# A fused FFT and SwiGLU kernel: the order of mirrored gate, gate, value and output matmuls within a unit

## The chip, the cores and the metric

The kernel runs on one core of a Trainium2 chip. The metric is the device time of one execution in microseconds (us); the time of a kernel is the median of its runs.

## The reference

The input `x` is 8 batches of 3008 rows of 256 numbers. The reference takes the real part of a two-dimensional FFT over the rows and the columns of each batch, and feeds the resulting 24064 rows to a SwiGLU block with 256 inputs, 1536 hidden units and 256 outputs:

```
attn = fft(fft(x, axis=1), axis=2).real        # 8 x 3008 x 256
g    = attn @ w_gate                            # 24064 x 1536
val  = attn @ w_val
out  = (silu(g) * val) @ w_out                  # 24064 x 256, float32
```

## The kernel before

**Pairs of rows.** For a real input, the FFT along the rows at row k and at row M-k (M = 3008) have the same cosine part and opposite sine parts. The kernel therefore computes the two parts once, `Pt` and `Qt` (128 x 512 in bf16, transposed: a column is a row of the sequence), and obtains both rows of a pair from them. The second FFT is folded into the weights: `Wp` and `Wq` are transformed gate and value weights for the two parts, and `Wm` is -2 times `Wq` apart from its first row, which is zero. The gate of the row itself is `Wp.P + Wq.Q`; the gate of the mirrored row is that sum plus `Wm.Q`.

**Tiles and units.** There are 12032 pairs. They are cut into 24 tiles `t` of 480, 512 or, for the last, 320 columns (`width`). A tile has 12 units `f`, one for each 128 of the 1536 hidden units, so there are 288 units. They are walked in order, with `prev` the unit before. What a unit `u` does for the row itself is called its direct half here; what it does for the mirrored row is its mirrored half.

The direct half is `part_a(u)`. TensorE runs two gate matmuls into a PSUM bank `g` (line 716) and then two value matmuls into a bank `v` (also line 716). ScalarE takes Silu of `g` (line 743), and VectorE multiplies it with `v` into `hp` (line 744). The mirrored half is `part_b(u)`. TensorE adds one matmul with `Wm` onto the same `g` and one onto the same `v` (line 753), ScalarE takes Silu of `g` again (line 761), and VectorE multiplies into `hm`, reversed (line 762).

**Split units.** In tiles 2 to 22 some units are split: f = 0, 2, 3, 5, 7, 9 up to tile 20 (`SPLIT`), and f = 0, 1, 2, 4, 5, 7, 8, 10, 11 in tiles 21 and 22 (`SPLIT_END`). A split unit has no mirrored value matmul. Its two value matmuls go into two banks of the pool `psV`, `e` = `Wp.P` and `o` = `Wm.Q`. VectorE forms `es` from `e` (line 731), then the direct value `vp` (line 733) and the mirrored value `vm` (line 735) from `o` and `es`. GpSimd does both multiplications (lines 736 and 758). `es` needs the first row of `Qt` on all partitions: at f = 0 a matmul with `sel` (line 856) and a copy by ScalarE into `bc` (line 859) put it there.

**Output matmuls.** When a tile's twelve units are through, `OWork` holds its output work: for each 128 rows, 12 matmuls of 256 columns with `hp` or `hm` as weights and `Wo` as the moving operand (line 676). `owork.run(4)` issues four of them; two such groups stand in every unit, so the output of tile t-1 is spread over the units of tile t. Twenty-four matmuls fill a bank of `psO`; ScalarE then copies it to `ev` (line 682), and DMAs on SyncE's queue store it (line 688). With eight output matmuls in a unit (four in the first, since the new `OWork` is made in the middle of f = 0), a bank is full after the first group of the units f = 3, 6, 9, and of f = 0 of the next tile.

**Other work.** GpSimd folds the input of later batches (lines 153 to 172) in steps tied to unit numbers. `whole_part` transforms half a batch into new `Pt` and `Qt` after certain units, mostly f = 4: matmuls at line 567, two copies by ScalarE (line 575) and additions by VectorE (line 580). Loads of `x` and stores of the output share SyncE's queue.

**What sets the order.** Each engine follows the order in which the Python code emits its instructions, and waits on semaphores. Buffers matter too. The PSUM pools `psG` and `psV` have three banks each and `psO` two; `sgv` (Silu results for GpSimd) and `vv` (`vp`, `vm`) have four buffers, `sg` three. A pool hands out the buffer that was given back first, counted in the order of the code, and whoever writes into it first waits for its last reader. The loop over units is, around the change:

```
        part_a(u)
        if owork:
            owork.run(4)
        if prev is not None:
            part_b(prev)
            if prev[1] == nF - 1:
                owork = OWork(prev[0], hts[prev[0]])
                owork.run(4)
        if owork and not (prev is not None and prev[1] == nF - 1):
            owork.run(4)
```

Of the kernel before, what the change touches and what calls it, by code (L numbers as in the profile page):

```python
# [12 lines left out]
F32 = mybir.dt.float32  # L13
I32 = mybir.dt.int32
BF16 = mybir.dt.bfloat16
AF = mybir.ActivationFunctionType
Alu = mybir.AluOpType
# [14 lines left out]
def kernel(  # L32
# [8 lines left out]
    nc = tc.nc  # L41
    B, M, D = x.shape
    Dff = moe_w_gate.shape[1]
    P = 128
# [4 lines left out]
    nF = Dff // P  # L49
    T = 512  # L50
# [6 lines left out]
    nT = len(wide)  # L57
# [9 lines left out]
    def width(t):  # L67
        return wide[t]
# [16 lines left out]
    Wm = const.tile([P, 2, Dff], BF16, name="Wm")  # L85
# [40 lines left out]
    def load_a(b, q):  # L126
        X3 = XA.rearrange("p a q d -> p a (q d)")
        return ([lambda h=h: q.dma_start(out=X3[LA * h:LA * (h + 1), 0:4, :],
                                         in_=up_block(b, JA - LA * h, LA)) for h in range(NA)] +
                [lambda a=a: q.dma_start(out=X3[:, 4 + a, :], in_=down_set(b, a, JA, LA, NA)) for a in range(4)])  # L130
# [129 lines left out]
    for i in range(6):  # L260
        ps = psO.tile([P, T], F32, name="o")
# [252 lines left out]
    def pq_tiles(t):  # L514
        if t not in ptile:
            w = width(t) + B if t == nT - 1 else T
            ptile[t] = (pqp if t < nT - 1 else const).tile([P, w], BF16, name="Pt")
            qtile[t] = (pqp if t < nT - 1 else const).tile([P, w], BF16, name="Qt")
        return ptile[t], qtile[t]
# [78 lines left out]
    def whole_part(b, part):  # L598
        transform(b, part, (0,))
        transform(b, part, (1,))  # L600
# [15 lines left out]
    sgp = ctx.enter_context(tc.tile_pool(name="sg", bufs=3))  # L616
    sgv = ctx.enter_context(tc.tile_pool(name="sgv", bufs=4))
# [75 lines left out]
    hts = {}  # L693
    state = {}
    owork = None
# [7 lines left out]
    def split(u):  # L703

        return 2 <= u[0] < nT - 1 and u[1] in (SPLIT if u[0] < t_end else SPLIT_END)

    def part_a(u):
        t, f = u
        w = width(t) + (B if t == nT - 1 else 0)
        fs = slice(f * P, (f + 1) * P)  # L710
        if f == 0:
            hts[t] = (hp.tile([P, nF, T + B], BF16, name="hp"), hp.tile([P, nF, T], BF16, name="hm"))
        Pt, Qt = pq_tiles(t)

        def mm(ps, Wt, gv, src, start, stop):
            nc.tensor.matmul(ps[:, :w], Wt[:, gv, fs], src[:, :w], start=start, stop=stop,  # L716
                             skip_group_check=True)

        g = psG.tile([P, T], F32, name="g")
        mm(g, Wp, 0, Pt, True, False)  # L720
        mm(g, Wq, 0, Qt, False, True)
        if split(u):
            e = psV.tile([P, T], F32, name="v")
            mm(e, Wp, 1, Pt, True, True)
            o = psV.tile([P, T], F32, name="v")
            mm(o, Wm, 1, Qt, True, True)
            sg = sgv.tile([P, T], F32, name="sgv")
            nc.scalar.activation(sg[:, :w], g[:, :w], AF.Silu)  # L728
            stt = nc.vector.scalar_tensor_tensor
            es = esp.tile([P, T], F32, name="es")  # L730
            stt(es[:, :w], bc[t][:, :w], w0[:, f:f + 1], e[:, :w], op0=Alu.mult, op1=Alu.add)  # L731
            vp = vvp.tile([P, T], F32, name="vv")
            stt(vp[:, :w], o[:, :w], -0.5, es[:, :w], op0=Alu.mult, op1=Alu.add)  # L733
            vm = vvp.tile([P, T], F32, name="vv")
            stt(vm[:, w - 1::-1], o[:, :w], 0.5, es[:, :w], op0=Alu.mult, op1=Alu.add)  # L735
            nc.gpsimd.tensor_tensor(hts[t][0][:, f, :w], sg[:, :w], vp[:, :w], op=Alu.mult)  # L736
            state[u] = (g, vm)
            return
        v = psV.tile([P, T], F32, name="v")
        mm(v, Wp, 1, Pt, True, False)  # L740
        mm(v, Wq, 1, Qt, False, True)
        sg = sgp.tile([P, T], F32, name="sg")
        nc.scalar.activation(sg[:, :w], g[:, :w], AF.Silu)  # L743
        nc.vector.tensor_tensor(hts[t][0][:, f, :w], sg[:, :w], v[:, :w], op=Alu.mult)  # L744
        state[u] = (g, v)

    def part_b(u):
        t, f = u
        w = width(t)
        Pt, Qt = pq_tiles(t)  # L750
        g, v = state.pop(u)
        for gv, ps in ((0, g), (1, v))[:1 if split(u) else 2]:
            nc.tensor.matmul(ps[:, :w], Wm[:, gv, f * P:(f + 1) * P], Qt[:, :w], start=False, stop=True,  # L753
                             skip_group_check=True)
        if split(u):
            sg = sgv.tile([P, T], F32, name="sgv")
            nc.scalar.activation(sg[:, w - 1::-1], g[:, :w], AF.Silu)  # L757
            nc.gpsimd.tensor_tensor(hts[t][1][:, f, :w], sg[:, :w], v[:, :w], op=Alu.mult)  # L758
            return
        sg = sgp.tile([P, T], F32, name="sg")  # L760
        nc.scalar.activation(sg[:, :w], g[:, :w], AF.Silu)  # L761
        nc.vector.tensor_tensor(hts[t][1][:, f, w - 1::-1], sg[:, :w], v[:, :w], op=Alu.mult)  # L762


    slot = {(b, part): max(first_tile[(b, part)] - 1, 0) * nF + 4 for b, part in jobs}
# [10 lines left out]
    for b in range(2, B, 2):  # L776
        u = slot[(b, 0)] - 1
# [8 lines left out]
    def run_loads(n):  # L786
        for _, fn in loads[:n]:
            fn()
        del loads[:n]

    def fold_step(what, i, unit):
        kind, b = what
        q, j = divmod(i, 7)
        if i == 0:
            run_loads(max((k + 1 for k, (w_, _) in enumerate(loads) if w_ == what), default=0))
        if j == 0:
            if kind == "A":
                queue[what] = fold_steps(nc.gpsimd, XA, *coef_a(b), q, slice(0, P))
            else:
                queue[what] = fold_steps(nc.gpsimd, XC, *coef_c(b), q, slice(64 if b == 1 else 0, P))  # L800
        queue[what].pop(0)()
        if q == 1 and j == 1:
            act_at.setdefault(max(unit + 2, 11), []).append(what)

    def load_next(what):
        kind, b = what
        if kind == "A":
            if b + 1 < B:
                loads.extend((("A", b + 1), fn) for fn in load_a(b + 1, nc.sync))
        else:  # L810
            b = b // 2 * 2 + 2
            if b < B:
                loads.extend((("C", b), fn) for fn in load_c(b, nc.sync) + load_c(b + 1, nc.sync))
# [5 lines left out]
    for jb in jobs[1:]:  # L819
        u = slot[jb]  # L820
# [28 lines left out]
    prev = None  # L849
    owork = None  # L850
    for i, u in enumerate(units):
        t, f = u
        if f == 0 and split((t, SPLIT[0])):
            ps = psG.tile([P, T], F32, name="g")
            w = width(t)
            nc.tensor.matmul(ps[:, :w], sel, pq_tiles(t)[1][:, :w], start=True, stop=True)  # L856
            bc.pop(t - 2, None)
            bc[t] = bcp.tile([P, T], F32, name="bc")
            nc.scalar.copy(bc[t][:, :w], ps[:, :w])
        for fn in before.pop(i, ()):  # L860
            fn()
        if i == 10:
            loads[0:0] = ((("A", 1), fn) for fn in load_a(1, nc.sync))
        run_loads(3)
        part_a(u)
        if owork:
            owork.run(4)
        if prev is not None:
            part_b(prev)
            if prev[1] == nF - 1:  # L870
                owork = OWork(prev[0], hts[prev[0]])
                owork.run(4)
        if owork and not (prev is not None and prev[1] == nF - 1):
            owork.run(4)
        for what, j in fold_at.get(i, ()):
            fold_step(what, j, i)
        for what in act_at.pop(i, ()):
            load_next(what)
        if i in job_at:
            whole_part(*job_at[i])  # L880
        prev = u
    while owork.steps:
        owork.run(8)
    part_b(prev)
    owork = OWork(prev[0], hts[prev[0]])
    owork.run(len(owork.steps))

# [29 lines left out]
```

## Time and profile before

| | |
|---|---|
| median of 3 runs | 693.22 us (692.69 to 694.37) |
| the profiled execution | 693.12 us, its span 691.4 us |
| TensorE matmul busy | 673.5 us, 97% of the span |
| GpSimd busy | 593.4 us, 86% |
| VectorE busy | 517.9 us, 75% |
| ScalarE busy | 433.4 us, 63% |
| granted TensorE clock | 0.997 of full speed |

The busy time of an engine is the union of its instructions' spans. The ends of matmuls are modelled, and consecutive matmuls overlap in the record: a matmul of 512 columns is listed with 0.38 us, while the next starts 0.216 us later. A short wait of TensorE is therefore seen not as idle time but in the distance from one start to the next.

### The profile page before, as it was taken

What the parts mean: (1) busy time and instruction counts of PE and PEld (TensorE: products, weight loads), DVE (VectorE), ACT (ScalarE), POOL (GpSimd) and SP (SyncE); (2) the same over time, 40 slices, a digit from 0 to 9 for tenths busy, and PEclk for the clock granted to TensorE, in tenths of its full rate; (3) what the DMA queues carried; (4) which work ended last, traced back from release to release, by engine and by line L of the source; (5) the groups of instructions that cost most, each with busy time, mean ns of one, the idle gap of its engine ahead of it and who ended that gap; (6) DMA issues with size and microseconds to landing.
All of it is one profiled execution on the core that took longest, in us unless ns stands there. A gap on an engine that the chain in (4) does not pass through costs nothing.

```text
span 691.4 us, 13273 instructions
## 1 busy us (share of the span) xinstructions
PE 673.5 (97%) x4369; PEld 414.4 (60%) x4369; DVE 517.9 (75%) x925; ACT 433.4 (63%) x765; POOL 593.4 (86%) x577
## 2 busy tenths in 40 slices
PE   7999979999999999999999999999999999999997
PEld 5446645566556566566665656655665656656676
DVE  8896657677768777777777778777877787788862
ACT  7676546566556566565665656655666656656663
POOL 8998999999999999999997989998999555658920
PEclk9999999999999999999999999999999999999999
DMA  9656362332413313324134111125111011111112
GB/s 225 113 78 131 101 142 74 96 99 61 131 37 90 110 31 105 89 68 132 47 82 117 45 34 46 32 58 140 43 36 46 32 41 37 46 32 47 47 47 70
DMA packets 45567, 52.55 MB, mean 76 GB/s; under 512 B 6290, under 2 KB 33466, under 8 KB 45498
## 3 DMA queue, kind: packets, MB, share of 16 engines
q1 hardware_dynamic: 42314, 49.35, 26.2%
q0 software_dynamic: 3184, 2.36, 2.4%
q8 instruction: 34, 0.56, 0.4%
q14 instruction: 35, 0.29, 0.2%
HBM read 29.39 MB, written 24.65 MB: 78 GB/s over the span
## 4 chain that ended last, share of the span: by engine, by line
PE 85%; DMA 4%; DVE 4%; issue 3%; POOL 1%; SPq 1%; ACT 1%; ACTq 0%; POOLq 0%; DVEq 0%
PE o L676 33%; PE v L716 17%; PE g L716 15%; PE g L753 8%; PE v L753 4%; PE g L567 3%; PE v L567 3%; DVE vv L735 2%; DMA XC<-in_x_dram 2%; DMA XC_108<-in_x_dram 1%; SPq L139 1%; DMA XA<-in_x_dram 1%; DVE vv L733 1%; DMA out_dram<-ev 1%; PE g L856 1%
## 5 line engine op out<-in xcount | busy, mean ns | idle before, releaser
L736 POOL TENSOR_TENSOR hp<-sgv,vv 128x512 bf16<-128x512 f32 (+1 forms) x132 | 167.8, 1272 | 49.8 <-DVE vv L733 38.4
L758 POOL TENSOR_TENSOR hm<-sgv,vv 128x512 bf16<-128x512 f32 (+1 forms) x132 | 167.3, 1272 | 8.5 <-ACT sgv L757 8.1
L676 PE MATMUL o<-Wo,hp 128*128 128x256 bf16 (+2 forms) x1140 | 170.6, 274 | 0.0
L676 PE MATMUL o<-Wo,hm 128*128 128x256 bf16 (+2 forms) x1140 | 169.6, 273 | 0.0
L676 PEld LDWEIGHTS <-hp 128*128 128x128 bf16 (+2 forms) x1140 | 112.3, 99 | 70.9 <-issue 11.3
L676 PEld LDWEIGHTS <-hm 128*128 128x128 bf16 (+2 forms) x1140 | 111.9, 98 | 64.8 <-issue 5.5
L731 DVE SCALAR_TENSOR_TENSOR es<-bc,w_85,v 128x512 f32<-128x512 f32 (+1 forms) x132 | 98.2, 744 | 51.3 <-PE v L716 51.0
L744 DVE TENSOR_TENSOR hp<-sg,v 128x512 bf16<-128x512 f32 (+2 forms) x156 | 103.7, 665 | 31.2 <-ACT sg L743 30.8
L761 ACT ACTIVATE sg<-g 128x512 f32<-128x512 f32 (+2 forms) x156 | 91.1, 584 | 43.1 <-PE g L753 43.0
L762 DVE TENSOR_TENSOR hm<-sg,v 128x512 bf16<-128x512 f32 (+2 forms) x156 | 103.2, 662 | 18.7 <-ACT sg L761 8.6
L743 ACT ACTIVATE sg<-g 128x512 f32<-128x512 f32 (+2 forms) x156 | 90.9, 583 | 41.5 <-PE g L716 39.6
L757 ACT ACTIVATE sgv<-g 128x512 f32<-128x512 f32 (+1 forms) x132 | 78.9, 598 | 53.9 <-PE g L753 41.3
L716 PE MATMUL v<-Pt,Wp 128*128 128x512 bf16 (+2 forms) x288 | 107.9, 375 | 1.6 <-DVE vv L735 1.6
L716 PE MATMUL g<-Pt,Wp 128*128 128x512 bf16 (+2 forms) x288 | 108.3, 376 | 1.0 <-ACT sgv L757 0.9
L716 PE MATMUL g<-Qt,Wq 128*128 128x512 bf16 (+2 forms) x288 | 108.0, 375 | 0.5 <-DVE Qt L580 0.5
L753 PE MATMUL g<-Qt,Wm 128*128 128x512 bf16 (+2 forms) x288 | 108.1, 375 | 0.0
L733 DVE SCALAR_TENSOR_TENSOR vv<-v,es 128x512 f32<-128x512 f32 (+1 forms) x132 | 91.1, 690 | 22.5 <-POOL hp L736 4.6
L728 ACT ACTIVATE sgv<-g 128x512 f32<-128x512 f32 (+1 forms) x132 | 78.7, 596 | 44.8 <-PE g L716 34.9
L735 DVE SCALAR_TENSOR_TENSOR vv<-v,es 128x512 f32<-128x512 f32 (+1 forms) x132 | 89.8, 681 | 8.1 <-POOL hm L758 5.2
L716 PEld LDWEIGHTS <-Wp 128*128 128x128 bf16 x576 | 56.4, 98 | 41.1 <-issue 4.5
L682 ACT COPY ev<-o 128x512 f32<-128x512 f32 x90 | 52.8, 587 | 30.9 <-PE o L676 29.7
L153 POOL TENSOR_TENSOR SDf<-XA 128x1024 f32<-128x1024 f32 x28 | 66.0, 2364 | 3.4 <-DMA XC<-in_x_dram 2.6
(173 smaller groups left out, 736.0 us busy)
## 6 DMA issues: line engine op xcount, KB each, us to landing
out_dram<-ev SPq DMA_DIRECT2D x96, 128.0 KB
XA<-in_x_dram SPq DMA_DIRECT2D x32, 256.0 KB
XA<-in_x_dram SPq DMA_DIRECT2D x112, 64.0 KB
XC<-in_x_dram SPq DMA_DIRECT2D x105, 32.0 KB
XC<-in_x_dram SPq DMA_DIRECT2D x28, 120.0 KB
out_dram<-ev SPq DMA_DIRECT2D x12, 120.0 KB
out_dram<-ev SPq DMA_DIRECT2D x10, 112.0 KB
XA<-in_x_dram SPq DMA_DIRECT2D x1, 1024.0 KB
```

The costliest lines, as they stand in the source:

```text
L676: nc.tensor.matmul(ps[:n, j, :], hts[minus][:, f, c:c + n], Wo[:, f, :], start=(f == 0), stop=(f == nF - 1))
L716: nc.tensor.matmul(ps[:, :w], Wt[:, gv, fs], src[:, :w], start=start, stop=stop, skip_group_check=True)
L731: stt(es[:, :w], bc[t][:, :w], w0[:, f:f + 1], e[:, :w], op0=Alu.mult, op1=Alu.add)
L733: stt(vp[:, :w], o[:, :w], -0.5, es[:, :w], op0=Alu.mult, op1=Alu.add)
L735: stt(vm[:, w - 1::-1], o[:, :w], 0.5, es[:, :w], op0=Alu.mult, op1=Alu.add)
L736: nc.gpsimd.tensor_tensor(hts[t][0][:, f, :w], sg[:, :w], vp[:, :w], op=Alu.mult)
L743: nc.scalar.activation(sg[:, :w], g[:, :w], AF.Silu)
L744: nc.vector.tensor_tensor(hts[t][0][:, f, :w], sg[:, :w], v[:, :w], op=Alu.mult)
L753: nc.tensor.matmul(ps[:, :w], Wm[:, gv, f * P:(f + 1) * P], Qt[:, :w], start=False, stop=True, skip_group_check=True)
L758: nc.gpsimd.tensor_tensor(hts[t][1][:, f, :w], sg[:, :w], v[:, :w], op=Alu.mult)
L761: nc.scalar.activation(sg[:, :w], g[:, :w], AF.Silu)
L762: nc.vector.tensor_tensor(hts[t][1][:, f, w - 1::-1], sg[:, :w], v[:, :w], op=Alu.mult)
```

## The change

For tile 0 (i < nF) the order stays as it was. From tile 1 on a unit is emitted as: the mirrored gate of the unit before with its Silu (`gate_b(prev)`; for a split unit also GpSimd's multiplication), four output matmuls, the two gate matmuls of the unit with their Silu (`gate_a(u)`), the mirrored value of the unit before with VectorE's multiplication (`value_b(prev)`, nothing for a split unit), the value matmuls and what follows from them (`value_a(u)`), four output matmuls. `part_a` is cut into `gate_a` and `value_a`, `part_b` into `gate_b` and `value_b`; what each of them computes is unchanged.

```diff
-    def part_a(u):
+    def gate_a(u):
...
         mm(g, Wq, 0, Qt, False, True)
+        sg = (sgv if split(u) else sgp).tile([P, T], F32, name="sgv" if split(u) else "sg")
+        nc.scalar.activation(sg[:, :w], g[:, :w], AF.Silu)
+        state[u] = (g, sg)
+
+    def value_a(u):
...
+        g, sg = state[u]
...
         if split(u):
             e = psV.tile([P, T], F32, name="v")
             mm(e, Wp, 1, Pt, True, True)
             o = psV.tile([P, T], F32, name="v")
             mm(o, Wm, 1, Qt, True, True)
-            sg = sgv.tile([P, T], F32, name="sgv")
-            nc.scalar.activation(sg[:, :w], g[:, :w], AF.Silu)
...
-    def part_b(u):
+    def mirror(u, gv, ps):
...
+    def gate_b(u):
+
+        t, f = u
+        w = width(t)
+        g, v = state[u]
+        mirror(u, 0, g)
         if split(u):
             sg = sgv.tile([P, T], F32, name="sgv")
             nc.scalar.activation(sg[:, w - 1::-1], g[:, :w], AF.Silu)
             nc.gpsimd.tensor_tensor(hts[t][1][:, f, :w], sg[:, :w], v[:, :w], op=Alu.mult)
-            return
-        sg = sgp.tile([P, T], F32, name="sg")
-        nc.scalar.activation(sg[:, :w], g[:, :w], AF.Silu)
-        nc.vector.tensor_tensor(hts[t][1][:, f, w - 1::-1], sg[:, :w], v[:, :w], op=Alu.mult)
+        else:
+            sg = sgp.tile([P, T], F32, name="sg")
+            nc.scalar.activation(sg[:, :w], g[:, :w], AF.Silu)
+            state[u] = (sg, v)
+
+    def value_b(u):
+        t, f = u
+        w = width(t)
+        sg, v = state.pop(u)
+        if not split(u):
+            mirror(u, 1, v)
+            nc.vector.tensor_tensor(hts[t][1][:, f, w - 1::-1], sg[:, :w], v[:, :w], op=Alu.mult)
...
-        part_a(u)
-        if owork:
-            owork.run(4)
-        if prev is not None:
-            part_b(prev)
+
+        if i < nF:
+            gate_a(u)
+            value_a(u)
+            if prev is not None:
+                gate_b(prev)
+                value_b(prev)
+        else:
+            gate_b(prev)
+            if owork:
+                owork.run(4)
+            gate_a(u)
+            value_b(prev)
             if prev[1] == nF - 1:
                 owork = OWork(prev[0], hts[prev[0]])
-                owork.run(4)
-        if owork and not (prev is not None and prev[1] == nF - 1):
+            value_a(u)
             owork.run(4)
```

More of the change, by code (lines that the diff above doesn't have):

```diff
@@ L721, in part_a, with mm @@
         mm(g, Wq, 0, Qt, False, True)
+        sg = (sgv if split(u) else sgp).tile([P, T], F32, name="sgv" if split(u) else "sg")
[3 more added lines that the diff above has]
+        t, f = u
+        w = width(t) + (B if t == nT - 1 else 0)
+        fs = slice(f * P, (f + 1) * P)
+        Pt, Qt = pq_tiles(t)
+        g, sg = state[u]
+        def mm(ps, Wt, gv, src, start, stop):
+            nc.tensor.matmul(ps[:, :w], Wt[:, gv, fs], src[:, :w], start=start, stop=stop,
+                             skip_group_check=True)
         if split(u):
@@ L741, in part_a @@
         mm(v, Wq, 1, Qt, False, True)
-        sg = sgp.tile([P, T], F32, name="sg")
-        nc.scalar.activation(sg[:, :w], g[:, :w], AF.Silu)
         nc.vector.tensor_tensor(hts[t][0][:, f, :w], sg[:, :w], v[:, :w], op=Alu.mult)
         state[u] = (g, v)
-    def part_b(u):
+    def mirror(u, gv, ps):
         t, f = u
         w = width(t)
[L750 to L754, printed above, removed]
+        nc.tensor.matmul(ps[:, :w], Wm[:, gv, f * P:(f + 1) * P], pq_tiles(t)[1][:, :w], start=False, stop=True,
+                         skip_group_check=True)
+    def gate_b(u):
[3 more added lines that the diff above has]
+        mirror(u, 0, g)
         if split(u):
@@ L758, in part_b @@
             nc.gpsimd.tensor_tensor(hts[t][1][:, f, :w], sg[:, :w], v[:, :w], op=Alu.mult)
-            return
-        sg = sgp.tile([P, T], F32, name="sg")
-        nc.scalar.activation(sg[:, :w], g[:, :w], AF.Silu)
-        nc.vector.tensor_tensor(hts[t][1][:, f, w - 1::-1], sg[:, :w], v[:, :w], op=Alu.mult)
+        else:
[3 more added lines that the diff above has]
+    def value_b(u):
+        t, f = u
+        w = width(t)
[3 more added lines that the diff above has]
+            nc.vector.tensor_tensor(hts[t][1][:, f, w - 1::-1], sg[:, :w], v[:, :w], op=Alu.mult)
     slot = {(b, part): max(first_tile[(b, part)] - 1, 0) * nF + 4 for b, part in jobs}
@@ L883 @@
         owork.run(8)
-    part_b(prev)
+    gate_b(prev)
+    value_b(prev)
     owork = OWork(prev[0], hts[prev[0]])
```

## The prediction

> **What bounds the kernel now.** First the page's busy line and the shares of its chain of waits, then TensorE's waits by who ended them (total, times, longest).
>
> ```profile
> PE 673.5 (97%) x4369; PEld 414.4 (60%) x4369; DVE 517.9 (75%) x925; ACT 433.4 (63%) x765; POOL 593.4 (86%) x577
> ...
> PE 85%; DMA 4%; DVE 4%; issue 3%; POOL 1%; SPq 1%; ACT 1%; ACTq 0%; POOLq 0%; DVEq 0%
> ```
>
> ```profile
> PE v L716 <- DVE vv L735: 4.1, 3, 2.0
> PE v L753 <- DVE hp L744: 2.0, 4, 0.8
> ```
>
> TensorE is the bound (97%). Since starts stand closer than the listed spans, I take its waits from start-to-start distances in its timeline: 216 ns after 512 columns, 109 ns after 256 (medians, 100 to 600 us). Distances beyond that sum to some 53 us in the span, two thirds of them before 100 us or around the transforms, which the change does not touch. The largest group is `e` to `o` of a split unit: 10.5 us in 46 waits. In tiles 3 to 20 it is 0.06 us at f=0 and 0.26 at f=3. This is the timeline of all engines around f=3:
>
> ```profile
> 310.16 0.68 DVE L735 SCALAR_TENSOR_TENSOR vv<-v,es 128x512 f32<-128x512 f32 x1
> 310.20 0.38 PE L716 MATMUL g<-Qt,Wq 128*128 128x512 bf16 x1
> ...
> 310.42 0.38 PE L716 MATMUL v<-Pt,Wp 128*128 128x512 bf16 x1
> ...
> 310.68 0.60 ACT L728 ACTIVATE sgv<-g 128x512 f32<-128x512 f32 x1 [0.55 <-PE g L716]
> ...
> 310.89 0.38 PE L716 MATMUL v<-Qt,Wm 128*128 128x512 bf16 x1
> ...
> 311.11 0.60 PE L676 MATMUL o<-Wo,hp 128*128 128x256 bf16 x4
> ...
> 311.74 0.59 ACT L682 COPY ev<-o 128x512 f32<-128x512 f32 x1 [0.46 <-PE o L676]
> ```
>
> The second value matmul starts 0.47 after the first: it needs the bank of unit 2's `o`, read until 310.84 by `vm`. The same lines give ScalarE's delays: Silu starts 0.476 after the second gate matmul (medians: 0.476 into `sgv`, 0.416 into `sg`), the eviction 0.309 after the last output matmul. Two more, from other places of ScalarE's and TensorE's timelines:
>
> ```profile
> 86.74 0.60 ACT L757 ACTIVATE sgv<-g 128x512 f32<-128x512 f32 x1 [2.23 <-POOL hp L736]
> ...
> 87.39 0.38 PE L716 MATMUL g<-Pt,Wp 128*128 128x512 bf16 x1 [0.90 <-ACT sgv L757]
> ...
> 93.27 0.60 ACT L728 ACTIVATE sgv<-g 128x512 f32<-128x512 f32 x1 [3.25 <-POOL hp L736]
> 93.76 0.59 ACT L761 ACTIVATE sg<-g 128x512 f32<-128x512 f32 x1
> ```
>
> TensorE goes on 0.65 after the start of a Silu that it waits for; queued ScalarE instructions start 0.49 apart (0.483 after an eviction).
>
> **What the Trainium skill says.** "TensorE: Matmul & The Clock Gate", Part 1: a warm matmul takes N/2.4 GHz + 2.5 ns, and an idle window of about 3.4 us halves the clock. The trace agrees: 216 ns, and near 91 us, after waits, 512 columns take 0.43. "ScalarE: Activation LUTs", What ACT_TABLE_LOAD costs: 186 ns + 0.833 N, queued ACTIVATEs overlapping by about 93 ns; for 512 that is 612, the trace has 597 and an overlap of 110. "Perfetto Trace Analysis", Per-engine timelines: ScalarE is strictly first-in-first-out, so whatever stands ahead of a Silu delays it. The trace shows that too (at f=2, 5, 8, 11 of most tiles the mirrored Silu is 0.21 to 0.27 late behind an eviction; today nobody on TensorE waits for it).
>
> **The change, part by part.** TensorE's instructions are the same in number and size. SyncE's queue keeps its order (loads, then stores behind evictions): nothing. On GpSimd and VectorE, `hm` of the unit before moves ahead of `hp` of this one; work is the same, and an adjacent swap is put at nothing under the cover of TensorE running a unit ahead; without it, one 1.23 us `hm` delays one `hp`.
>
> *Removed: waits for banks of `psV`.* The mirrored value now comes before the unit's own value, so the bank of unit 1 is given back before `e` of unit 2 is taken; `o` of unit 3 then gets unit 2's `e` bank, read one unit earlier. By the durations above (`es` to `vp` 0.88, `vp` to `vm` 0.61) every `e`, `o` and `v` has 0.5 us or more in hand. After 100 us that is 7.7 us of `e` to `o`, plus 0.26 at a gate matmul near 633 us: **-7.9**.
>
> *Added: the mirrored gate waits for a fresh Silu.* It accumulates onto the bank that the direct Silu reads. Today 3 us lie between the gate matmuls and it; afterwards only the two value matmuls and four output matmuls (and the mirrored value, if `prev` is not split). Let 0 be the start of the mirrored gate of `prev`. The second gate matmul starts at 0.216+0.436+0.216=0.868. The next mirrored gate is due 0.216+0.432+0.436=1.084 later, at 1.952; or at 2.168 when `prev` is not split.
> - No eviction: the Silu starts at 0.868+0.476=1.344 and releases at 1.99 (split unit) or 1.93 (not split). Late only for split after split: 0.04.
> - Eviction (f=3, 6): mirrored Silu at 0.476; `ev` could start at 0.216+0.327+0.309=0.852, waits until 0.96; Silu at 1.442, release 2.09: **0.137 late**, `prev` being split in both.
> - f=9: `prev` is not split: 1.382+0.647=2.03 against 2.168, nothing.
> - f=0: the `sel` matmul and `bc` go first: `bc` at 0.20, mirrored Silu 0.683, `ev` 1.166, Silu 1.649, release 2.296 against 2.168: **0.128**.
>
> A tile of tiles 3 to 20 loses 0.40: 18 x 0.40 = 7.2. Tile 2 adds 0.1 at f=0, tile 21 0.7 (five split-after-split, three evictions), tile 22 0.95, tile 23 0.35: **+9.4**. Behind a waiting mirrored gate, everything on TensorE queues.
>
> *The mirrored value* waits for `hp` of `prev`: Silu end plus one 0.68 us VectorE instruction, 1.8 after the second gate matmul, due 2.17 after: nothing, 0.3 in hand.
>
> *The stretch 80 to 98 us.* GpSimd is continuously busy from 76 us (folds of two batches), `sgv` buffers run out, and ScalarE stands still behind GpSimd. Keeping GpSimd's times: the Silu of f=3 starts at 86.74, so the mirrored gate after it goes at 87.4 (TensorE waits from 84.15), the next at 90.55, 93.9 and 97.9; `g` of f=8 at 100.7, where the kernel before has it at 99.66: **+1.05**. The half clock lies beside these waits in both. Bounds: -1 (the 1.06, 2.13 and 1.81 us waits shrink as `o` has a free bank) to +3 (one more GpSimd fold of 2.35 in the way).
>
> *GpSimd's other late releases.* After 100 us four mirrored Silus are late by GpSimd: 0.13, 0.28, 0.29, 0.79. The slack ahead of the next Silu covers about 0.4: **+0.5**; bounds 0 and, if each of the twenty-odd ScalarE waits on GpSimd (some 12 us listed after 100 us) reached TensorE, +8.
>
> Sum: -7.9+9.4+1.05+0.5 = **+3.0** on the profiled execution's 693.1 (span 691.4 and 1.7 around it); the median is 693.22, so **696**.
>
> **Rivals.**
> 1. *The Silu is in time* (faster). It only has to start 0.14 earlier, e.g. if the eviction slips behind the Silu or ScalarE drains faster than 0.483 apart. For: the deficit is small. Against: program order is `ev` first, and 0.483 is the measured minimum. Then -7.9+1.05+0.5: 687.
> 2. *Both cancel* (no change): release 0.02 sooner than two places show, and 80 to 98 us neutral: 694.
> 3. *GpSimd decides* (much slower). From 60 to 480 us it is over 90% busy; the mirrored gate has lost its 3 us of tolerance, so each late `sgv` buffer stops TensorE. It decides once `hp` of two split units before ends after the Silu's own time in most tiles. Against: today only four such cases after 100 us. Price up to +8 more: 704.
> 4. *The change does less than it says*: the order is fixed by the code, so only tile 0 is excepted; no chance of its own.
>
> **Numbers.** A measurement of this kernel tells about 0.3% (2.1 us) from no change: 691.1 to 695.3 is "same". Forecast 0.50 (694.5 to 698), rival 1 0.15, rival 2 0.15, rival 3 0.20. Same gets rival 2 and a part of the forecast, less 0.01 each way: 0.22; faster 0.17 (rival 1 and strays); slower 0.61. The range 690 to 702 leaves out most of rival 1 and the far end of rival 3, 0.2 together.
>
> **What would show it.** Right: `e` to `o` distances at 216 ns after 100 us; 0.25 from the last output matmul to the mirrored gates of units 3, 6 and 0 (0.11 without a wait), released by ScalarE; Silu and `ev` on the chain in their places. Wrong: mirrored gates without waits (rival 1); GpSimd on the chain in many tiles (rival 3); waits of the mirrored value for `hp`, which I put at nothing.

## The result: 1.2% slower

| | before | changed |
|---|---|---|
| median | 693.74 us (692.69 to 694.37, 4 runs) | 701.96 us (700.06 to 702.84, 4 runs) |
| the profiled execution | 693.12 us, span 691.4 us | 702.84 us, span 701.1 us |
| GpSimd busy | 593.4 us | 593.1 us |
| granted TensorE clock | 0.997 | 0.992 |

The ratio of the times is 1.0116, with a 95% interval of 1.0091 to 1.0142. The kernel lost 8.2 us. The prediction had +3: the result lies outside its forecast of 694.5 to 698, and 0.04 us inside its range of 690 to 702.

The page of the changed kernel, its busy line and the shares of the chain of waits:

```profile
PE 682.3 (97%) x4369; PEld 414.1 (59%) x4369; DVE 516.0 (74%) x925; ACT 424.1 (60%) x765; POOL 593.1 (85%) x577
...
PE 87%; DVE 3%; DMA 2%; POOL 2%; issue 2%; SPq 1%; ACT 1%; DVEq 0%; ACTq 0%; POOLq 0%
```

The work is the same (4369 matmuls, GpSimd within 0.3 us), and TensorE is the bound as before. The 9 us more of "busy" PE are mostly waits: a matmul that starts 0.15 late leaves no gap in this record, since listed spans overlap. What does show as idle time stands in TensorE's waits (total, times, longest):

```profile
PE g L761 <- ACT sgv L723: 4.5, 5, 2.0
PE g L761 <- ACT sg L723: 2.8, 2, 2.4
PE v L761 <- DVE hp L755: 2.0, 4, 0.8
```

Line 761 is the mirrored matmul, line 723 the direct Silu, line 755 the multiplication into `hp` on VectorE; further down, line 734 is the value matmuls, 772 and 776 the mirrored Silu, 749 and 773 GpSimd's multiplications into `hp` and `hm`. The first two rows are new: before, no mirrored gate waited for the direct Silu. The third stands as before. The row that led the list then, value matmuls held up by `vm`, is gone.

Now f=3 of tile 11 in the changed kernel, TensorE and ScalarE in the timeline of all engines (start, duration, engine, line, operation, output and inputs; in brackets idle time just before, and who ended it). It answers to the f=3 that the prediction showed of before:

```profile
346.33 0.38 PE L761 MATMUL g<-Qt,Wm 128*128 128x512 bf16 x1
...
346.81 0.60 ACT L772 ACTIVATE sgv<-g 128x512 f32<-128x512 f32 x1 [0.70 <-PE g L761]
...
347.20 0.38 PE L716 MATMUL g<-Qt,Wq 128*128 128x512 bf16 x1
...
347.30 0.58 ACT L682 COPY ev<-o 128x512 f32<-128x512 f32 x1
347.42 0.38 PE L734 MATMUL v<-Pt,Wp 128*128 128x512 bf16 x1
...
347.63 0.38 PE L734 MATMUL v<-Qt,Wm 128*128 128x512 bf16 x1
...
347.76 0.62 ACT L723 ACTIVATE sgv<-g 128x512 f32<-128x512 f32 x1
...
347.85 0.60 PE L676 MATMUL o<-Wo,hp 128*128 128x256 bf16 x4
...
348.43 0.38 PE L761 MATMUL g<-Qt,Wm 128*128 128x512 bf16 x1
```

Three things can be read here. The two value matmuls of the split unit start 0.21 apart where the kernel before has 0.47: that wait is gone. The Silu (347.76) stands behind the eviction (347.30) and starts 0.56 after its gate matmul (347.20), where 0.476 is usual. And the mirrored gate starts at 348.43, while the four output matmuls from 347.85 on leave TensorE free at 347.85 + 4 x 0.109 = 348.29: it is 0.15 late, 0.67 after the start of the Silu. There is no bracket, since the record has no gap there; only the distance tells.

In tile 9 the wait at the same place is ten times as long. TensorE, ScalarE and GpSimd there, in the changed kernel:

```profile
284.52 4.67 POOL L153 TENSOR_TENSOR SDf<-XA 128x1024 f32<-128x1024 f32 x2
...
289.15 1.27 POOL L749 TENSOR_TENSOR hp<-sgv,vv 128x512 bf16<-128x512 f32 x1
...
290.46 0.60 ACT L723 ACTIVATE sgv<-g 128x512 f32<-128x512 f32 x1 [1.28 <-POOL hp L749]
...
291.10 0.38 PE L761 MATMUL g<-Qt,Wm 128*128 128x512 bf16 x1 [1.37 <-ACT sgv L723]
```

Two folds of the input (4.67 us) stand ahead of GpSimd's `hp` of unit 0. The direct Silu of f=3 wants the `sgv` buffer which that `hp` reads, starts only at 290.46, and TensorE stands until 291.10, 1.53 us by distances. The kernel before, same place, has the same two folds:

```profile
277.77 4.69 POOL L153 TENSOR_TENSOR SDf<-XA 128x1024 f32<-128x1024 f32 x2
...
282.05 0.60 ACT L728 ACTIVATE sgv<-g 128x512 f32<-128x512 f32 x1 [0.55 <-PE g L716]
...
282.41 1.28 POOL L736 TENSOR_TENSOR hp<-sgv,vv 128x512 bf16<-128x512 f32 x1
...
283.73 0.60 ACT L757 ACTIVATE sgv<-g 128x512 f32<-128x512 f32 x1
```

There the direct Silu of f=3 starts at 282.05, ahead of that `hp`, and only the mirrored Silu of f=2 comes right after its end (283.69). On TensorE nobody waits for that one for 3 us. The difference is the order in which `sgv` buffers are taken. Before, it is direct 0, mirrored 0, direct 2, *direct 3*, mirrored 2; with four buffers, direct 3 gets the one that `hm` of unit 9 of the tile before has read. Afterwards it is direct 0, mirrored 0, direct 2, *mirrored 2, direct 3*, and direct 3 gets the buffer of direct 0. The wait at f=3 of tile 5 (0.39) comes about in the same way.

The third long wait, 0.58 at f=6 of tile 8, is of another kind. The direct Silu of f=6 writes `sg`, which GpSimd doesn't read. But the mirrored Silu of f=5 and the eviction stand ahead of it on ScalarE, and that mirrored Silu has waited for GpSimd:

```profile
268.81 0.60 ACT L772 ACTIVATE sgv<-g 128x512 f32<-128x512 f32 x1 [1.13 <-POOL hm L773]
...
269.30 0.58 ACT L682 COPY ev<-o 128x512 f32<-128x512 f32 x1
...
269.77 0.62 ACT L723 ACTIVATE sg<-g 128x512 f32<-128x512 f32 x1
...
270.43 0.38 PE L761 MATMUL g<-Qt,Wm 128*128 128x512 bf16 x1 [0.41 <-ACT sg L723]
```

**Where the 8 us lie.** Waits on TensorE, each measured as the distance from start to start beyond what the same matmuls take without a wait:

| | predicted | measured |
|---|---|---|
| `e` to `o` and value banks after 100 us, removed | -7.9 | -7.9 (none left) |
| mirrored gates behind Silu and eviction | +9.4 | +11.0 |
| stretch around 90 us (76 to 112 us) | +1.05 | +2.3 (7.5 before, 9.8 after) |
| GpSimd's later releases (tiles 5, 8, 9: 0.39, 0.58, 1.53; small ones) | +0.5 | +2.3 |
| sum | +3.0 | +7.7 |

The second row takes every such wait up to 0.15 (in tiles 22 and 23 up to 0.37, with three evictions or short matmuls there), and 0.27 of two mirrored values; the fourth takes what goes beyond 0.15 in the other tiles.

The third row isn't waits alone. The granted clock is 0.50 from 90.2 to 93.6 us in the kernel before, and 0.50 from 89.1 to 92.5 and once more from 99.4 to 102.8 us in the changed kernel. By distances, the matmuls in these stretches take 1.7 us more than at full clock before, and 3.1 us more after. So about 1.4 of the 2.3 is the second stretch at half clock, and only about 0.8 is longer waits.

The spans differ by 9.7. A further 1.67 of that arises before the first Silu (26.37 us before, 28.04 after), in work that the change doesn't touch: from 14 to 18 us the granted clock is 0.57 in the changed kernel's trace and 1.00 in the other. Some 0.3 I cannot assign. Without that start 8.0 remain, near the 8.2 of the medians.

### The profile page after: what moved, and what is told of

It reads as the page before. It is cut to its first block, busy times and chain, and to the rows that moved or that the text cites. A ratio compares the mean times of both kernels' runs of the same rounds, so it can differ in the third digit from the quotient of the medians.

```text
span 701.1 us, 13284 instructions
## 1 busy us (share of the span) xinstructions
PE 682.3 (97%) x4369; PEld 414.1 (59%) x4369; DVE 516.0 (74%) x925; ACT 424.1 (60%) x765; POOL 593.1 (85%) x577
## 4 chain that ended last, share of the span: by engine, by line
PE 87%; DVE 3%; DMA 2%; POOL 2%; issue 2%; SPq 1%; ACT 1%; DVEq 0%; ACTq 0%; POOLq 0%
PE o L676 33%; PE g L716 16%; PE v L734 16%; PE g L761 9%; PE v L761 4%; PE g L567 3%; PE v L567 3%; DMA XA<-in_x_dram 1%; DMA out_dram<-ev 1%; DVE vv L746 1%; PE g L421 1%; PE v L421 1%; SPq L139 1%; PE g L879 1%; PE v L543 1%
## 5 line engine op out<-in xcount | busy, mean ns | idle before, releaser
L744 DVE SCALAR_TENSOR_TENSOR es<-bc,w,v 128x512 f32<-128x512 f32 (+1 forms) x132 | 97.6, 739 | 0.3 <-PE v L734 0.3
L761 PE MATMUL v<-Qt,Wm 128*128 128x512 bf16 (+2 forms) x156 | 58.2, 373 | 2.0 <-DVE hp L755 2.0
L734 PE MATMUL v<-Qt,Wq 128*128 128x512 bf16 (+2 forms) x156 | 58.3, 374 | 0.0
```

What stands on the lines that cost most here:

```text
L761: nc.tensor.matmul(ps[:, :w], Wm[:, gv, f * P:(f + 1) * P], pq_tiles(t)[1][:, :w], start=False, stop=True, skip_group_check=True)
```

## Experiments

All are compared with runs of the kernel before on the same chip (medians 694.07, 694.31 and 694.3 us for the three groups of runs). Diffs are against the changed kernel.

| kernel | median us | ratio to before, 95% interval |
|---|---|---|
| `changed_again` | 700.59 | 1.0090 [1.0071, 1.0110] |
| `evict_late` | 696.44 | 1.0031 [1.0022, 1.0039] |
| `outputs_first` | 692.00 | 0.9969 [0.9955, 0.9982] |
| `value_mirror_last` | 702.83 | 1.0120 [1.0101, 1.0139] |
| `changed_sgv6` | 698.73 | 1.0066 [1.0048, 1.0084] |
| `outputs_first_sgv6` | 696.69 | 1.0035 [1.0019, 1.0051] |
| `before_sgv6` | 694.38 | 1.0001 [0.9990, 1.0013] |
| `before_again` | 694.58 | 1.0005 [0.9995, 1.0014] |
| `outputs_first_5_5` | 690.48 | 0.9938 [0.9917, 0.9960] |
| `outputs_first_value_last` | 693.34 | 0.9993 [0.9981, 1.0004] |
| `gate_behind` | 694.11 | 0.9990 [0.9979, 1.0002] |

### The changed kernel and the kernel before, once more

`changed_again` and `before_again` are the two kernels unaltered.

> The changed kernel once more, beside the others on one chip. The account of its profile says that about 1.7 us of the 9.7 us between the two profiled spans lies before the first unit, where the code is the same. Theory (mirrored gate waits for a fresh Silu, GpSimd's late releases come through): 7 to 8 us slower than the kernel before, with the start's share averaged out. If the start belongs to the change: 9 to 10 us slower.

> The kernel before once more, for its profile: in the one shown, its first Silu starts at 26.4 us, in five profiles of other orders 0.5 to 1.7 us later, with the same instructions ahead of it. Theory (chance of the first loads): between 26.4 and 28, and a time equal to the kernel before. Otherwise the start belongs to the change.

Measured: the changed kernel is at 700.59 us, 6.5 us slower than the kernel before on the same chip; 7 to 8 were expected, and 8.2 measured at first (the intervals of the two ratios overlap). After 112 us it shows the same waits in the same places (0.15 in every tile, 1.54 in tile 9, 0.59 in tile 8). Between 76 and 112 us it has only one stretch at half clock (98.3 to 101.7 us), as the kernel before has, and loses 1.5 us there instead of 2.3. The kernel before is at 694.58, and in this profile its first Silu stands 1.66 us later than in the first one. The later start is therefore no property of the change. It goes with a granted clock of 0.64 from 14 to 18 us, where the first profile has 1.00; but `changed_sgv6` below starts as late (27.88) with a clock of 1.00 there, so the clock isn't the only cause.

### The eviction behind the Silu

`evict_late` issues the copy of a full output bank, and its stores, after the unit's direct Silu.

```diff
             gate_b(prev)
+            later = []
             if owork:
-                owork.run(4)
+                owork.run(4, later)      # the eviction is kept for later
             gate_a(u)
+            for fn in later:
+                fn()
             value_b(prev)
```

> The changed kernel, with the copy of a full output bank (and its stores) put behind the Silu of the unit's own gate in ScalarE's order, instead of ahead of it. Theory A (the eviction ahead of the Silu makes the mirrored gate late by 0.15 us at f = 0, 3 and 6): those waits go, 0.04 stays where a split unit follows a split one, so 60 waits of 0.11 to 0.15, some 8 us, are won: 693 to 695, within 1.5 us of the kernel before. Rival B (the wait is the Silu's own length and the eviction has no part in it): 701 to 702 as before. Rival C (GpSimd's late buffers are the larger share): at most 3 us are won.

Measured: 696.44 us, 4.2 less than the changed kernel beside it, where some 8 were expected. This is f=3 of tile 11 (its lines stand 5 further on; line 683 is the eviction):

```profile
345.56 0.38 PE L721 MATMUL g<-Qt,Wq 128*128 128x512 bf16 x1
...
346.04 0.60 ACT L728 ACTIVATE sgv<-g 128x512 f32<-128x512 f32 x1 [0.27 <-PE g L721]
...
346.21 0.60 PE L676 MATMUL o<-Wo,hp 128*128 128x256 bf16 x4
346.53 0.58 ACT L683 COPY ev<-o 128x512 f32<-128x512 f32 x1
...
346.69 0.38 PE L766 MATMUL g<-Qt,Wm 128*128 128x512 bf16 x1
```

The Silu starts 0.48 after its gate matmul, ahead of the eviction, and the mirrored gate is 0.04 late (346.21 + 4 x 0.109 = 346.65). The 0.15 at f=0 and f=6 are gone: the eviction ahead of the Silu is the cause of the wait that recurs in every tile. In most tiles without GpSimd trouble this version gains 0.27 us on the kernel before, where the changed kernel loses 0.14. But it won half of what was to be won. GpSimd's late releases hold TensorE for longer now, presumably since it arrives there earlier:

```profile
287.31 0.60 ACT L728 ACTIVATE sgv<-g 128x512 f32<-128x512 f32 x1 [2.40 <-POOL hp L754]
...
287.96 0.38 PE L766 MATMUL g<-Qt,Wm 128*128 128x512 bf16 x1 [2.01 <-ACT sgv L728]
```

This is tile 9 again: 2.17 by distances instead of 1.53; the one in tile 5 grew from 0.39 to 0.86. Behind the wait in tile 9 the granted clock is 0.50 for 3.4 us (289.0 to 292.4). Tile 9 as a whole takes 3.4 us longer than in the kernel before, against 1.5 in the changed kernel, so the clock has a share in what was not won, at least in the profiled execution.

### The output matmuls ahead of the mirrored gate

`outputs_first` puts all eight output matmuls between the value matmuls and the next mirrored gate.

```diff
-            gate_b(prev)
             if owork:
                 owork.run(4)
+            gate_b(prev)
             gate_a(u)
```

> The changed kernel with two statements swapped: the first four output matmuls of a unit stand ahead of the mirrored gate instead of behind it, so the mirrored gate comes 0.44 us later after its Silu; the order gate, mirrored value, value, four output matmuls stays. Theory A (0.44 us more in hand covers the 0.15 us behind an eviction): no waits at the mirrored gate but those behind GpSimd over 0.4, and the waits for value banks stay away too: 10 to 12 us faster than the changed kernel, 690 to 692, faster than the kernel before by 2 to 4 us. Rival C (GpSimd decides): the waits only move to the same places, 697 or more. Rival D (eight output matmuls in a row make their weights late): distances over 0.109 between them, slower.

Measured: 692.00 us, 2.1 us faster than the kernel before, where 2 to 4 were expected. This is f=3 of tile 11:

```profile
341.31 0.38 PE L716 MATMUL g<-Qt,Wq 128*128 128x512 bf16 x1
...
341.56 0.60 ACT L772 ACTIVATE sgv<-g 128x512 f32<-128x512 f32 x1
...
341.96 1.04 PE L676 MATMUL o<-Wo,hp 128*128 128x256 bf16 x8
342.05 0.61 ACT L723 ACTIVATE sgv<-g 128x512 f32<-128x512 f32 x1
...
342.83 0.38 PE L761 MATMUL g<-Qt,Wm 128*128 128x512 bf16 x1
```

The Silu starts at 342.05, so its bank is free near 342.72; the output matmuls last until 341.96 + 8 x 0.109 = 342.83, and there the mirrored gate starts, without a wait. A quiet tile takes 0.30 us less than before. So nothing is wrong with freeing the value banks: what the change pays is that only four output matmuls lie between the value matmuls and the mirrored gate. In tile 9 the wait behind GpSimd is still there, 2.11 us.

Part of the 2.1 us may come by the clock. The profiled execution has no stretch at half clock around 90 us, where the kernel before has one, and the mean granted clock of the 15 runs is 0.998, of the kernel before beside them 0.996. How much of the gain this is was not separated.

### The mirrored value back behind the value matmuls

`value_mirror_last` keeps the mirrored gate where the change put it and undoes the other half.

```diff
             gate_a(u)
+            value_a(u)
             value_b(prev)
             if prev[1] == nF - 1:
                 owork = OWork(prev[0], hts[prev[0]])
-            value_a(u)
             owork.run(4)
```

> The changed kernel with the mirrored value put back behind the unit's own value; the mirrored gate stays at the unit's start. This takes away the part of the change that frees the value banks. Theory A (the two parts add up): waits of e to o come back, 0.26 us or more at f = 3 of each tile and small ones at f = 0, and the waits at the mirrored gate stay, somewhat less where both fall into one unit: 5 to 8 us slower than the changed kernel, 707 to 710. Rival E (freeing the value banks gave nothing, the 7.9 us would have gone in any case because TensorE now waits elsewhere): 702, and no e to o distances over 0.22.

Measured: 702.83 us, only 2.2 more than the changed kernel, where 5 to 8 were expected. The wait from `e` to `o` is back at f=3 of tiles 2 to 20; this is tile 11:

```profile
345.26 0.38 PE L734 MATMUL v<-Pt,Wp 128*128 128x512 bf16 x1
...
345.60 0.68 DVE L785 TENSOR_TENSOR hm<-sg,v 128x512 bf16<-128x512 f32 x1
345.61 0.62 ACT L723 ACTIVATE sgv<-g 128x512 f32<-128x512 f32 x1
345.73 0.38 PE L734 MATMUL v<-Qt,Wm 128*128 128x512 bf16 x1
...
345.94 0.60 PE L676 MATMUL o<-Wo,hp 128*128 128x256 bf16 x4
...
346.38 0.38 PE L761 MATMUL g<-Qt,Wm 128*128 128x512 bf16 x1
```

`e` to `o` is 0.47 again, but the mirrored gate now follows the fourth output matmul directly (345.94 + 4 x 0.109 = 346.38). While TensorE waits for the bank, the Silu catches up. The two waits cover each other at f=3, so their prices don't add: 0.26 replaces 0.15. At f=0 and f=6 the 0.15 stay.

### Six buffers for `sgv`

```diff
-    sgv = ctx.enter_context(tc.tile_pool(name="sgv", bufs=4))
+    sgv = ctx.enter_context(tc.tile_pool(name="sgv", bufs=6))
```

This was done to the changed kernel, to `outputs_first`, and to the kernel before. If the ring of buffers is what makes the Silus wait, two more take that wait away.

> The changed kernel with six buffers of Silu results for GpSimd (sgv) instead of four; nothing else. In the changed order the buffers go round as direct 0, mirrored 0, direct 2, mirrored 2, direct 3, so the Silu of f = 3 needs the buffer of unit 0's direct Silu, read by GpSimd's multiplication of unit 0; in the order before, it got one that was read earlier. Theory F (this is why GpSimd's releases now stop TensorE): the long waits at the mirrored gate after f = 3 and 6 in tiles 5, 8, 9 (0.4 to 1.5 us) go, and a part of the 2.3 us lost between 76 and 112 us: 3 to 5 us faster than the changed kernel, 696 to 698; the 0.15 us behind evictions stay. Rival (GpSimd is simply overloaded there, any buffer count fills up, or the vv buffers take over): 700 or more.

> The kernel before with six sgv buffers. It tells what the buffers are worth without the change. Theory F: after 112 us its TensorE does not wait behind GpSimd, so only the stretch of 84 to 98 us can gain: 0 to 4 us faster, 690 to 694. If it gains as much as the changed kernel does, the buffers have nothing to do with the new order.

> Output matmuls first (the mirrored gate 0.44 us later) and six sgv buffers together. Theory A and F together: no waits at the mirrored gate after 112 us, value banks free, and less lost between 76 and 112 us: 687 to 690, 4 to 7 us faster than the kernel before. Rival (buffers bring nothing where the gate already has room): 692 as with four buffers.

Measured: the changed kernel's three long gate waits become as short as all others (1.53, 0.58 and 0.39 to 0.15). In tile 9 the direct Silu of f=3 now starts ahead of `hp` of unit 0:

```profile
285.73 0.62 ACT L723 ACTIVATE sgv<-g 128x512 f32<-128x512 f32 x1
...
286.29 1.27 POOL L749 TENSOR_TENSOR hp<-sgv,vv 128x512 bf16<-128x512 f32 x1
...
286.40 0.38 PE L761 MATMUL g<-Qt,Wm 128*128 128x512 bf16 x1
```

So the buffer was the cause of those waits. The kernel before gains nothing (694.38). By the medians the changed kernel gains 1.9 us, less than the 3 to 5 expected, and the intervals of the two ratios overlap; the traces are the firmer evidence. Not all of the wait was won. One of 0.43 is new at f=3 of tile 15, and part moved to the next resource, in `changed_sgv6` to the mirrored value near 92 and 99 us:

```profile
92.03 0.38 PE L761 MATMUL v<-Qt,Wm 128*128 128x512 bf16 x1 [2.79 <-DVE hp L755]
...
99.20 0.38 PE L761 MATMUL v<-Qt,Wm 128*128 128x512 bf16 x1 [1.21 <-DVE hp L755]
```

`outputs_first_sgv6` is 2.4 us slower than the kernel before, where with four buffers it was 2.1 us faster, against expectation. Its timeline in tile 9:

```profile
290.26 1.26 POOL L773 TENSOR_TENSOR hm<-sgv,vv 128x512 bf16<-128x512 f32 x1
...
291.56 0.69 DVE L748 SCALAR_TENSOR_TENSOR vv<-v,es 128x512 f32<-128x512 f32 x1 [1.71 <-POOL hm L773]
...
292.30 0.73 PE L567 MATMUL v<-Tab,BBa 128*128 128x376 bf16 x2 [1.65 <-DVE vv L748]
```

With Silu buffers to spare, the four `vv` buffers run out: VectorE stands 1.71 us behind GpSimd's `hm`, keeps the value bank, and the transform that needs the bank waits. Afterwards TensorE is slow, by the table of windows for the same kernel (window; its length, busy time and instructions of each engine; granted clock, DMA share, GB/s):

```profile
280.00:288.00 8.00, 7.95 (x53) 5.15 (x53) 6.52 (x10) 4.86 (x10) 7.92 (x8) 1.00 0.35 99
...
292.20:296.00 3.80, 3.70 (x12) 1.07 (x12) 2.27 (x8) 0.47 (x1) 3.80 (x4) 0.52 0.15 40
296.00:300.00 4.00, 3.78 (x17) 1.98 (x16) 2.26 (x4) 1.23 (x3) 3.72 (x5) 0.60 0.00 0
```

The granted clock is 0.52 and 0.60 in the 8 us after the wait, where it was 1.00 before it: 0.48 of 3.8 us and 0.40 of 4.0 us are some 3.4 us of lost clock, twice the wait. This is not a matter of the one profile. The mean granted clock is 0.988 to 0.993 in all 11 runs of this kernel, and 0.994 to 0.999 in the 40 of the kernel before beside them.

### Five and five

`outputs_first_5_5` is `outputs_first` with five buffers for `sgv` and five for `vv`.

> Output matmuls first, with five sgv and five vv buffers instead of four and four. With six sgv and four vv, the trace shows the wait going on to VectorE's mirrored value, which had no vv buffer, and from there to a value bank (1.65 us before a transform in tile 9, then a stretch at half clock). Theory F (both rings need one more): no wait of over 0.3 us behind GpSimd in tiles 5, 8 and 9, the stretch of 76 to 112 us neutral: 688 to 690. Rival G (GpSimd's backlog there is longer than one buffer covers, so the wait only moves again): 692 to 697.

Measured: 690.48 us, ratio 0.9938 [0.9917, 0.9960]: faster than both kernels, the fastest of the series, and just above the 688 to 690 expected. The long waits in tile 9 are gone. Others came in their place; these are among TensorE's waits:

```profile
PE g L761 <- ACT sg L723: 3.1, 1, 3.1
...
PE o L676 <- POOL hp L749: 1.3, 2, 1.1
PE g L567 <- POOL CEa L166: 1.2, 2, 0.6
```

The first stands near 95 us, within the expectation's stretch of 76 to 112 us. Output matmuls wait for an `hp` that isn't made, transforms for input that isn't folded; neither is a wait for a free buffer of these two rings. The profiled span (690.2) is no shorter than that of `outputs_first` (689.3), but it has two stretches of 3.4 us at half clock (from 95.7 and from 177.7 us) where the other has none. So what the buffers bring on top is read from the two ratios alone, whose intervals overlap a little, and the six runs here range from 687.37 to 692.33.

### Which half of the gain, and the gate ahead

`outputs_first_value_last` has the eight output matmuls first and the mirrored value behind the value matmuls (both diffs above together). `gate_behind` starts a unit with its own gate:

```diff
+            gate_a(u)
             gate_b(prev)
             if owork:
                 owork.run(4)
-            gate_a(u)
             value_b(prev)
```

> Output matmuls first, but the mirrored value behind the unit's own value, so that the value banks are given back as late as in the kernel before. It tells what freeing the banks is worth where the mirrored gate has room. Theory: in the changed kernel the waits for banks at f = 3 (0.26) and the waits at the mirrored gate (0.15) cover each other, so taking the first back cost only 2 us; here nothing covers them: 0.32 us for each of tiles 3 to 20 and more in 21 and 22, 6 to 8 us slower than output matmuls first, 698 to 700. Rival E (freeing the banks gains nothing by itself): 692.

> Another order: gate, mirrored gate of the unit before, four output matmuls, mirrored value, value, four output matmuls. The direct Silu stands ahead of the mirrored one in ScalarE's order, as in the kernel before, and over 1.5 us lie between the gate matmuls and the mirrored gate; the value banks are freed early. Theory A: no waits at the mirrored gate, at most 0.2 us at a mirrored value of f = 4 (VectorE, whose multiplication for the mirrored row now comes later): 690 to 693. As direct 2, direct 3 stand ahead of mirrored 2, 3 in the sgv ring again, the GpSimd waits of tiles 5 to 9 should be as few as in the kernel before (theory F); with rival G they stay.

Measured: 693.34 and 694.11 us. In the first the 0.26 from `e` to `o` is back in every tile, and a quiet tile gains 0.05 instead of 0.30; yet it is only 1.3 us slower than `outputs_first`, where 6 to 8 were expected. By the start of the direct Silus it loses less at the two places where GpSimd is late, 0.27 instead of 1.2 from tile 5 to 6 and 1.05 instead of 1.8 from tile 9 to 10. `gate_behind` has no such waits of the gate, gains 0.14 to 0.26 per quiet tile, and still ends with the kernel before: the mirrored value waits 0.13 to 0.15 in some units for `hp`, and 0.57 and 1.24 us are lost behind GpSimd at 275 and 290 us.

## Why the prediction was right in direction and too small

The direction, the two large terms and their places came out of the working; the sum was 4.7 us short of the measured one. That the range held the first result, by 0.04 us, was luck, though the repeat at 700.59 us lies well inside it. Two slips in the working weigh little: the parts listed under +9.4 add up to 9.3, and the waits of the kernel before that it puts at 53 us are about 45 when I add them up with its 216 and 109 ns and other widths in proportion.

**Value banks.** Right, to the number, in the waits: -7.9, no `e` to `o` wait is left after 112 us. What that is worth in time depends on the other waits: taken back alone it cost 2.2 us (`value_mirror_last`) and 1.3 us (`outputs_first_value_last`).

**The mirrored gate.** Right in mechanism and places: f=0, 3 and 6 in tiles 3 to 20, nothing at f=9, 0.04 for split after split. The size was a little low: 0.15 each instead of 0.128 to 0.137, that is 0.45 instead of 0.40 a tile, 18 x 0.45 = 8.1 instead of 7.2; the other 0.7 of the row's difference lies in tiles 2 and 21 to 23 and in the two mirrored values. The Silu started as worked out (1.43 after the mirrored gate; 1.442 predicted); TensorE went on 0.67 after it and not 0.647. With so little margin a delay of 0.02 weighs. `evict_late` and `outputs_first` show the cause by taking it away in two ways. That ScalarE is strictly first-in-first-out, which the prediction took from the Trainium skill ("Perfetto Trace Analysis", Per-engine timelines), is what decided here: the Silu starts 0.48 after its gate matmul with the eviction behind it, and 0.56 with the eviction ahead.

**The adjacent swap at nothing.** This is the step that failed. I looked at the swap of `hm` and `hp` on GpSimd's queue and not at what the same swap does to the ring of `sgv` buffers: it moved the wait for `hp` of unit 0 from a mirrored Silu to the direct Silu of f=3, for which TensorE now waits. So the sum under "GpSimd's other late releases", which counted only *mirrored* Silus that were late in the old order, gave +0.5; measured +2.3. Of this, 1.6 lie in the direct Silus of f=3 in tiles 5 and 9 (0.39 and 1.53, less the 0.15 of the eviction each). The 0.43 of tile 8 come from a late mirrored Silu, the kind that was counted, and are about as large as the +0.5. `changed_sgv6`, which takes these waits away, shows that the buffers cause them; that the median gains 1.9 and not the whole goes with the waits that moved. The bounds of 0 to +8 held.

**The stretch around 90 us.** +1.05 predicted, +2.3 measured, within its bounds of -1 to +3. I had kept GpSimd's times as they were and moved the waits. The waits of 2.0 and 2.4 us near 88 and 99 us are in the list above; with six buffers, waits of 2.79 and 1.21 us stand at the mirrored value instead. The working said that the half clock lies beside these waits in both kernels. It lies there once before and twice after, and that is about 1.4 of the 2.3. In `changed_again`, with one such stretch, the loss is 1.5, nearer to the forecast.

**The mirrored value waiting for `hp`: nothing.** Right in the changed kernel apart from two of 0.13 to 0.14; with the mirrored value one group earlier (`gate_behind`) that margin is used up.

**The rivals.** "Both cancel" fell with the 0.15. "The Silu is in time" did not come about; with the eviction moved it nearly does, and is then worth 4.2 us, less than the 9 us between it and the forecast; the longer waits behind GpSimd stand against it. "GpSimd decides" (704) was nearest in time but not in kind: after 112 us it decides in three tiles, and it has a part around 90 us; in most tiles the eviction does. That the buffer order belongs to GpSimd's part was missing in it as well.

**What limits all these orders.** The window table of the kernel before, from 112 to 480 us (columns as above, with the engines named in the answer's head: PE, PEld, DVE, ACT, POOL):

```profile
112.00:480.00 368.00, 366.35 (x2367) 223.77 (x2366) 281.54 (x487) 233.00 (x411) 354.08 (x324) 1.00 0.28 79
```

GpSimd is busy 354 of 368 us, 96%. It looks as if an order that saves TensorE 0.3 us in a tile only lets it arrive earlier where GpSimd is late: `evict_late`, `outputs_first` and `gate_behind` gain 0.14 to 0.30 in a quiet tile, which would be up to 5 us over 18 tiles, and end at +2.4, -2.1 and -0.2 us against the kernel before. This is argued and not shown: less work on GpSimd was not tried, and the stretches at half clock, which differ from run to run, were not separated from it.

## What to carry to other kernels

Before an accumulation is moved closer to the reader of its bank, add up that reader's queue: here one eviction of 0.48 us ahead of a Silu used up the margin, and four matmuls of 0.109 us moved across the boundary gave it back. A repeat of both kernels is worth having before a difference of a few us is split into terms: here 1.7 us of start and 1.4 us of clock came with single executions. When a reordering changes the order in which a ring of buffers is taken, work out anew whose reader each writer waits for; equal work and equal counts say nothing about it. And when a second engine is 96% busy beside the bound, read gains per stage, since what is won in the quiet stages may be handed back in the busy ones.

## What the runs showed of the hardware

- The cost of a wait on TensorE isn't only its length: in `outputs_first_sgv6` successive pairs of matmuls of 376 columns start 0.67 to 0.74 us apart after the wait, at a granted clock of 0.52, and 0.41 to 0.43 before it, at 1.00. The Trainium skill ("TensorE: Matmul & The Clock Gate", Part 1) gives an idle window of about 3.4 us for the halving, and the prediction took this as confirmed. The traces do not confirm it: TensorE had been idle for only 1.65 us in one piece here, and for 2.13 us by distances in the kernel before, where the clock is 0.50 from 90.2 us on. Waits as long can pass without it: `outputs_first` has 2.06 and 2.11 us near 97 and 286 us and no such stretch. What decides between the two these traces don't tell.
- Executions of one and the same kernel can differ by 1.66 us before the first Silu (`before_again` and the kernel before), as much as a fifth of the effect studied, and in the number of stretches of 3.4 us at half clock (two in the changed kernel around 90 us, one in its repeat). Two spans are better compared from the first common instruction on, and with their granted clocks beside them.
- TensorE starts 0.65 to 0.67 us after the start of a 0.60 to 0.62 us Silu that it waits for, about 0.05 after its end.
